# A mixer and MLP block on one core: tile 1's first product in two column halves, and another order of the work

## The chip, the cores and the metric

The kernel runs on one core of one Trainium2 chip. The metric is the device time of one execution in microseconds (us), the median over several runs; lower is better. A core has five engines that run side by side and meet at semaphores: TensorE (PE, matrix products and transposes into PSUM), VectorE (DVE), ScalarE (ACT, activations), GpSimd (POOL) and SyncE (SP, which issues most DMAs here). PEld in a profile is TensorE's loading of weights.

## The reference

With S = 2048 tokens, D = 512 and F = 1792, all in bf16:

```python
h = _gelu(_layernorm(x, axis=-1) @ w1)
c = D // 4
g0 = jnp.pad(h[:, :, 0*c:1*c], ((0, 0), (1, 0), (0, 0)))[:, :S, :]
g1 = jnp.pad(h[:, :, 1*c:2*c], ((0, 0), (0, 1), (0, 0)))[:, 1:, :]
g2 = jnp.pad(h[:, :, 2*c:3*c], ((0, 0), (2, 0), (0, 0)))[:, :S, :]
g3 = jnp.pad(h[:, :, 3*c:   ], ((0, 0), (0, 2), (0, 0)))[:, 2:, :]
hs = jnp.concatenate([g0, g1, g2, g3], axis=-1) @ w2
x1 = x + hs
h2 = _gelu(_layernorm(x1, axis=-1) @ w3) @ w4
return x1 + h2
```

Each quarter of h's columns is shifted by 1, -1, 2 or -2 tokens before the second product. A layer norm comes ahead of the first and of the third product. The tanh form of gelu is used.

## The kernel before

The tokens are cut into 16 tiles of 128. Everything stays in on-chip memory between loading and storing; x and the four weights are loaded once.

Per tile there are two layer norms, numbered q: q = 0 to 15 for the first (of x), q = 16 to 31 for the second (of x1, tile q-16). Statistics come from VectorE (L409, L411) or, for q in STAT_ACT, from ScalarE (L388, L393) with small VectorE steps (L398 to L405). GpSimd raises the variance to the power -0.5 (L416, rstd). The normalisation is done by VectorE (L437), by ScalarE (L446) or by GpSimd (L449), as the table NORM says; the last two need a factor nmr first (L442, placed by NMR). The normalised tile is then turned, to have its columns on the partitions: by TensorE with a copy out of PSUM (`pe_transpose`, L482 and L490, the copy placed by EVAC) or by a DMA transpose on SP's queue (L455).

The products, by the names that the order uses:

- up1: first product and gelu, for a group of tiles (GROUPS[1]). In general (L586, L601) the result has tokens along the free dimension, as the shifts need it. Tiles 0 and 1 (NAT) are done the other way round: the product is by rows (`mm_up_rows`, L520, x's tile as weights), a gelu with rstd as its scale (L539) writes hn, and TensorE turns hn (`h_transpose`, L557), from which it is copied to hT (L563, engine by HEV). So these tiles' products need not wait for rstd. Tile 0 (SPLIT) has its first half of the normalised columns turned and multiplied before the second: steps sa, sb and ra, rb, where the halves are of the contraction, not of the output.
- mix: the shifted second product (L626) and x1 = x + hs (L633 or L637). Mix t needs h of tiles t-1, t and t+1.
- up2: third product and gelu for a group of tiles (GROUPS[2], L586 and L601).
- down: fourth product (L655), addition of x1 (L663) and output DMA (L666). The last tile goes in three pieces (TAIL).

The third product of a tile needs the second layer norm of that tile, and that needs its mix. PSUM is used as three pairs of banks (y_ps: up1, up2, most transposes) and two single banks (o_ps: mix, down, h_transpose), each taken in turn.

The order of TensorE's work is written out in SCRIPT ("ty" is a TensorE transpose by number q, "th" the transpose of hn, "up2:0" a group's number). The order of the loads is written out in LOADS: "x4-5" is a DMA of two tiles, "a" and "b" are halves of a weight's rows, "@act" is issued by ScalarE, "tp11" is a DMA transpose with a fixed place among the loads, which counts only if TensorE does not do that transpose. For the other engines a planner (`order`, `place`) gives each step a due time, counted back from TensorE's order (starting at DUE, with BIAS added), and places the steps by a model of durations, waits and landings. The outcome is a fixed list for each engine; at run time each instruction waits for semaphores only, and an engine takes its list in order.

Of the kernel before, what the change touches and what calls it, by code (L numbers as in the profile page):

```python
# [6 lines left out]
P = 128  # L7
ACT_F = mybir.ActivationFunctionType
# [17 lines left out]
class Program:  # L26
# [2 lines left out]

    HOP = {"pe": 200.0, "dve": 155.0, "act": 220.0, "pool": 120.0, "sp": 70.0}  # L30
    LOOK = {"dve": 300.0, "act": 300.0}
    DUE = 252723.0
    BEGIN = {"sp": 30.0, "act": 150.0, "pe": 400.0, "dve": 150.0, "pool": 450.0}
    ENTRY = 1900.0
    COLD, RESTART = 4300.0, 800.0
# [219 lines left out]
        self.seq = out  # L255
        return out

GROUPS = {1: (1, 1, 1, 1, 1, 1, 2, 2, 2, 2, 2), 2: (2, 2, 4, 4, 4)}
NORM = {4: "act", 5: "act", 6: "act", 10: "act", 11: "pool", 12: "pool", 13: "act", 15: "act", 18: "pool", 20: "pool", 21: "pool", 22: "pool", 24: "act", 28: "act", 30: "pool"}
EVAC = {1: "both", 2: "dve", 3: "dve", 7: "both", 9: "dve", 10: "both", 11: "both", 13: "both", 16: "dve", 17: "both", 19: "both", 20: "dve", 22: "both", 23: "dve", 24: "dve", 25: "dve", 28: "dve", 31: "dve"}  # L260
STAT_ACT = (1, 6, 8, 9, 12, 21, 22, 23, 27, 28, 29)
TAIL = (256, 128, 128)
NMR = {0: "pool", 1: "pool", 3: "pool", 5: "pool", 7: "pool", 9: "pool", 10: "pool", 12: "pool", 13: "pool", 14: "pool", 17: "pool", 18: "pool", 19: "pool", 21: "pool", 22: "pool", 23: "pool", 27: "pool", 30: "pool"}
NAT = (0, 1)
SPLIT = (0,)
HEV = {2: "dve", 5: "dve", 6: "dve"}
BIAS = {}
LOADS = """
x0 w1a w1b x4-5 w2b tp2 x3 w2a x6-7 w3b x8 w3a x1@act x9 x2@act x11 tp16 w4a x10 tp11 w4b tp9 x12-14 x15
"""  # L270
SCRIPT = """
warm:8 sa:0 sb:0 ty:1 ra:0 rb:0 up1:1 ty:2 th:0-1 up1:2 mix:0 ty:4 ty:3 mix:1 up1:3 ty:5 up1:4 mix:2 up1:5
mix:3 ty:17 mix:4 up2:0 up1:6 up2:1 mix:6 down:1 mix:5 up1:7-8 mix:8 mix:7 up1:9 mix:10 down:0 down:2 mix:9
up1:10 mix:12 mix:11 up2:2 mix:13 down:3 down:6 mix:14 up2:3 mix:15 down:4-5 down:7 down:11 down:9-10 up2:4
down:8 down:12 down:14 down:13 down:15
"""

def bass_standalone__mixer_s_mlp__prompt_kernel(nc, x, w1, w2, w3, w4, out):
    B, S, D = x.shape
    F = w3.shape[1]  # L280
    assert B == 1 and D == 4 * P and S % 512 == 0 and F % (2 * P) == 0 and S >= 1024
    NT, DC, FC = S // P, D // P, F // P
# [10 lines left out]
    with ExitStack() as es:  # L293
        sb = lambda name, shape, dt: es.enter_context(nc.sbuf_tensor(name, shape, dt))
        x_sb = sb("x_sb", [P, NT, D], BF16)
        x1_sb = sb("x1_sb", [P, NT, D], BF16)
        xnT = sb("xnT", [P, DC, S], BF16)
        hT = sb("hT", [P, DC, HTW], BF16)
        h2T = sb("h2T", [P, FC, S], BF16)
        w1_sb = sb("w1_sb", [P, DC, D], BF16)  # L300
# [3 lines left out]
        ident = sb("ident", [P, P], BF16)  # L304
# [26 lines left out]
        def pair_rv(p, v):  # L331
            return [(("y", p, 0), v), (("y", p, 1), v)]
# [180 lines left out]
        def mm_up_rows(t):  # L513
            p, v = next_pair()
            k = NAT.index(t)

            def part(c0, c1):
                def f(e):
                    for dc in range(c0, c1):
                        ins = e.matmul(y_ps[:, p, 0:D], xnT[:, dc, P * t : P * (t + 1)], w1_sb[:, dc, :],  # L520
                                       start=(dc == 0), stop=(dc == DC - 1))
                    return ins

                return f

            if t in SPLIT:
                for hh in (0, 1):
                    cs = range(2 * hh, 2 * hh + 2)
                    pg.add("pe", f"rows{t}_{hh}", part(2 * hh, 2 * hh + 2),
                           reads=[(("w1", c), 0) for c in cs] + [(("xT", t, c), 1) for c in cs],  # L530
                           writes=[pair_rv(p, v)[hh]], dur=2 * 215.8)
                    if hh == 0:
                        yield
            else:
                pg.add("pe", f"rows{t}", part(0, DC),
                       reads=[(("w1", c), 0) for c in range(DC)] + [(("xT", t, c), 1) for c in range(DC)],
                       writes=pair_rv(p, v), dur=DC * 215.8)
            pg.add("act", f"gelur{t}",
                   lambda e: e.activation(hn[:, k, :], y_ps[:, p, 0:D], ACT_F.Gelu_apprx_tanh,  # L539
                                          scale=rstd[:, t : t + 1]),  # L540
                   reads=pair_rv(p, v) + [(("rstd", t), 0), (("warm",), 1)], writes=[(("hn", t), 0)], dur=50 + D * 0.833)
            yield

        def h_transpose(t, pair):
            g = group_of[1, t]
            how = HEV.get(t, "act")
            k = NAT.index(t)
            if pair:
                b, v = next_pair()
                res, dst = pair_rv(b, v), y_bf[:, b, 0:D]  # L550
            else:
                b, v = next_bank()
                res, dst = [(("o", b), v)], o_bf[:, b, 0:D]

            def f(e):
                for c in range(DC):
                    ins = e.transpose(dst[:, P * c : P * (c + 1)], hn[:, k, P * c : P * (c + 1)], ident[:])  # L557
                return ins

            pg.add("pe", f"th{t}", f, reads=[(("hn", t), 0), (("ident",), 1)], writes=res, dur=225)  # L560
            to, frm = hT[:, :, 2 + P * t : 2 + P * (t + 1)], dst.rearrange("p (c s) -> p c s", s=P)
            pg.add(how, f"evh{t}",
                   (lambda e: e.activation(to, frm, ACT_F.Copy)) if how == "act" else  # L563
                   (lambda e: e.tensor_copy(to, frm)),
                   reads=res, writes=[(("h", j, g), 0) for j in range(DC)],
                   dur=(60 + 0.82 * D) if how == "act" else (75 + 0.51 * D))


        def mm_up(layer, g):
            t0, n = groups[layer][g]  # L570
# [34 lines left out]
        def run(gen):  # L605
            for _ in gen:
                pass
# [82 lines left out]
        for step in SCRIPT.split():  # L690
            kind, n = step.split(":")
            a, _, b = n.partition("-")
            steps += [(kind, n) for n in (range(int(a), int(b or a) + 1) if kind != "warm" else [int(n)])]
        steps = [s for s in steps if s[0] not in ("th", "tz") or s[1] in NAT]
        pe_tp = {n for kind, n in steps if kind in ("tp", "ty", "sa")}
        queues = {"sp": [], "act": []}
        for i, item in enumerate(LOADS.split()):
# [10 lines left out]
        for kind, n in steps:  # L708
            if kind == "warm":
                warm_pe(n)  # L710
            elif kind in ("sa", "ra"):
                halves[kind[0], n] = pe_transpose(n, n, True) if kind == "sa" else mm_up_rows(n)
                next(halves[kind[0], n])
            elif kind in ("sb", "rb"):
                next(halves[kind[0], n])
            elif kind in ("tp", "ty"):
                run(pe_transpose(n % NT, n, kind == "ty"))
            elif kind in ("th", "tz"):
                h_transpose(n, kind == "tz")
            elif kind == "mix":  # L720
                mm_mix(n)
            elif kind == "down":
                mm_down(n)
            else:
                for _ in mm_up(int(kind[2]), n):
                    pass
# [103 lines left out]
```

## Time and profile before

| | us |
|---|---|
| median of 4 runs | 135.76 |
| the 4 runs | 135.68, 135.37, 135.84, 135.90 |
| the profiled execution | 135.68 |
| its span in the trace | 134.3 |

Busy times by stretch of the span, in us:

| stretch | PE | PEld | DVE | ACT | POOL | GB/s moved |
|---|---|---|---|---|---|---|
| 0 to 5 | 4.36 | 1.95 | 2.55 | 3.33 | 1.66 | 234 |
| 5 to 10 | 4.61 | 2.70 | 3.84 | 3.82 | 2.16 | 378 |
| 10 to 15 | 5.00 | 3.87 | 4.84 | 4.55 | 1.91 | 256 |
| 15 to 20 | 5.00 | 3.78 | 4.73 | 4.70 | 3.06 | 226 |
| 20 to 25 | 5.00 | 4.47 | 4.33 | 2.77 | 3.40 | 143 |

How to read it: the profile shows one execution. An engine's busy time is that of its instructions; the ends of matmuls are modelled, and a matmul overlaps the next, so a matmul's own length in the timeline is longer than the time by which it moves the next one. In the timeline a line gives the start, the length, engine, line of the code, operation, output and inputs with their shapes, how many instructions are merged in the line, and in square brackets the idle time before it and what ended it. The chain of waits goes back from the last instruction to what released each step. TensorE's clock was granted in full throughout (1.0).

Landings of the loads, each as issue plus time to landing in the trace, in us: x0 2.5, x1 2.8, x2 4.3, w1b 5.8, x4-5 6.5, w2b 7.2, x3 7.5, w2a 8.2, x6-7 9.0, w3b 11.2, w3a 13.9.

### The profile page before, as it was taken

How to read it: one execution, taken by the hardware profiler on the slowest of the kernel's cores; microseconds unless marked ns; L12 is line 12 of the kernel's file. 1: busy time of each engine (PE TensorE's matmuls, PEld its weight loads, DVE VectorE, ACT ScalarE, POOL GpSimd, SP SyncE). 2: the span in 40 equal slices, each digit the busy share in tenths (PEclk: the TensorE clock that was granted, in tenths of full speed). 3: DMA queues.
4: the chain of work that ended last, by engine and by line, in shares of the span. 5: the costliest groups of instructions: out<-in, count | busy, mean ns of one | idle time of the engine just before them, and what ended most of it. 6: DMA issues, size and time to landing. Idle time of an engine off the chain costs nothing.

```text
span 134.3 us, 2025 instructions
## 1 busy us (share of the span) xinstructions
PE 131.4 (98%) x792; PEld 72.8 (54%) x792; DVE 52.0 (39%) x140; ACT 58.4 (43%) x90; POOL 25.8 (19%) x59
## 2 busy tenths in 40 slices
PE   8989999999999999999999999999999999999994
PEld 3468688885576446444444444444444444444463
DVE  3889999404947737700053500062222200012222
ACT  5698995669394303775520366600000155520000
POOL 2534467600865301300010310010000000000000
PEclk9999999999999999999999999999999999999999
DMA  6999399599057532111003110004112100001112
GB/s 187 347 388 362 60 299 160 105 289 239 6 111 82 118 79 77 39 39 39 5 0 78 39 39 0 0 0 85 39 39 72 45 0 0 0 5 39 39 39 78
DMA packets 21897, 12.32 MB, mean 92 GB/s; under 512 B 14464, under 2 KB 21376, under 8 KB 21888
## 3 DMA queue, kind: packets, MB, share of 16 engines
q1 hardware_dynamic: 21168, 11.80, 33.6%
q10 hardware_dynamic: 720, 0.39, 1.0%
q8 instruction: 6, 0.10, 0.3%
q14 instruction: 3, 0.02, 0.0%
HBM read 6.82 MB, written 2.10 MB: 66 GB/s over the span
## 4 chain that ended last, share of the span: by engine, by line
PE 98%; ACT 1%; DVE 0%; issue 0%; POOLq 0%; ACTq 0%
PE y_ps L586 45%; PE o_ps L655 36%; PE o_ps L626 10%; PE o_ps L679 3%; PE y_ps L520 2%; PE y_ps L482 1%; ACT hn L539 1%; PE o_ps L557 0%; DVE o_sb L663 0%; POOLq L815 0%; ACTq L779 0%
## 5 line engine op out<-in xcount | busy, mean ns | idle before, releaser
L586 PE MATMUL y_ps<-xnT,w_sb 128*128 128x256 bf16 (+2 forms) x424 | 62.6, 307 | 0.0
L586 PEld LDWEIGHTS y_ps<-xnT,w_sb 128*128 128x128 bf16 x424 | 39.0, 98 | 23.4 <-DVE xnT L490 0.3
L655 PE MATMUL o_ps<-w_sb,h2T 128*128 128x512 bf16 (+2 forms) x252 | 49.2, 355 | 0.0
L601 ACT ACTIVATE h2T<-y_ps 128x1024 bf16<-128x1024 f32 (+1 forms) x29 | 28.6, 993 | 42.6 <-PE y_ps L586 42.6
L655 PEld LDWEIGHTS o_ps<-w_sb,h2T 128*128 128x128 bf16 x252 | 23.6, 98 | 25.2
L663 DVE TENSOR_TENSOR o_sb<-o_ps,x_sb 128x512 bf16<-128x512 f32 (+2 forms) x18 | 11.4, 632 | 40.0 <-PE o_ps L655 39.8
L416 POOL TENSOR_TENSOR rstd<-mv,neghalf 128x1 f32<-128x1 f32 x21 | 11.6, 554 | 42.6 <-DVE mv L411 38.6
L626 PE MATMUL o_ps<-w_sb,hT 128*128 128x512 bf16 x64 | 16.1, 379 | 0.0
L409 DVE BATCH_NORM_STATS2 st<-x_sb 128x6 f32<-128x512 bf16 x21 | 14.2, 675 | 2.2 <-DMA x_sb<-in_x_dram 2.0
L637 DVE TENSOR_TENSOR x_sb<-o_ps,x_sb 128x512 bf16<-128x512 f32 x10 | 6.9, 686 | 12.7 <-PE o_ps L626 12.7
L633 DVE SCALAR_TENSOR_TENSOR x_sb<-o_ps,x_sb 128x512 bf16<-128x512 f32 x6 | 4.1, 690 | 16.8 <-PE o_ps L626 16.8
L601 ACT ACTIVATE hT<-y_ps 128x1024 bf16<-128x1024 f32 (+1 forms) x9 | 7.4, 826 | 6.3 <-PE y_ps L586 6.2
L416 POOL TENSOR_TENSOR rstd<-vpe,neghalf 128x1 f32<-128x1 f32 x11 | 6.0, 549 | 18.8 <-DVE vpe L405 18.7
L626 PEld LDWEIGHTS o_ps<-w_sb,hT 128*128 128x128 bf16 x64 | 6.0, 98 | 5.5
L437 DVE TENSOR_SCALAR xn_buf<-x_sb,mv,rstd 128x512 bf16<-128x512 bf16 x15 | 7.0, 468 | 4.8 <-POOL rstd L416 4.6
L446 ACT ACTIVATE xn_buf<-x_sb,nmr,rstd 128x512 bf16<-128x512 bf16 x8 | 6.5, 811 | 5.2 <-DVE nmr L442 3.2
L393 ACT ACTIVATE junk<-x_sb 128x512 bf16<-128x512 bf16 x11 | 6.8, 622 | 2.7 <-DVE x_sb L633 2.7
L449 POOL TENSOR_SCALAR xn_buf<-x_sb,rstd,nmr 128x512 bf16<-128x512 bf16 x7 | 5.3, 763 | 0.8 <-DVE nmr L442 0.4
L679 PE MATMUL o_ps<-zeros 128*128 128x512 bf16 x8 | 3.6, 630 | 0.6 <-POOLq L815 0.6
L411 DVE BATCH_NORM_AGGREGATE mv<-st 128x2 f32<-128x9 f32 x21 | 4.0, 191 | 0.2
L388 ACT ACTIVATE junk<-x_sb 128x512 bf16<-128x512 bf16 x5 | 3.1, 622 | 0.3 <-DMA x_sb<-in_x_dram 0.3
L482 PEld LDWEIGHTS y_ps<-ident,xn_buf 128*128 128x128 bf16 x28 | 2.3, 111 | 1.3 <-issue 0.6
(35 smaller groups left out, 30.7 us busy)
## 6 DMA issues: line engine op xcount, KB each, us to landing
w_sb<-in_w_dram SPq DMA_DIRECT2D x4, 896.0 KB, 6.6
out_dram<-o_sb SPq DMA_DIRECT2D x15, 128.0 KB, 1.7
w_sb<-in_w_dram SPq DMA_DIRECT2D x4, 256.0 KB, 4.9
x_sb<-in_x_dram SPq DMA_DIRECT2D x7, 128.0 KB, 5.3
x_sb<-in_x_dram SPq DMA_DIRECT2D x2, 256.0 KB, 5.2
xnT<-xn_buf SPq DMA_TRANSPOSE x25, 2.5
x_sb<-in_x_dram SPq DMA_DIRECT2D x1, 384.0 KB, 4.9
x_sb<-in_x_dram ACTq DMA_DIRECT2D x2, 128.0 KB, 3.2
```

Source lines behind the costliest of these rows:

```text
L393: (lambda d: (lambda e: e.activation(d, src, ACT_F.Square, accum_out=sums[:, q, 1:2])))(junk[:, b, :]),
L409: pg.add("dve", f"bnst{q}", lambda e: e.bn_stats(st9[:, q, 0:6], src), reads=rs, writes=[(("st", q), 0)], dur=605)
L416: lambda e: e.tensor_tensor(col(rstd), var, neghalf[:], ALU.pow),
L437: lambda e: e.tensor_scalar(dst, src, mv[:, q, 0:1], rstd[:, q : q + 1], ALU.subtract, ALU.mult),
L446: f = lambda e: e.activation(dst, src, ACT_F.Identity, bias=nmr[:, q : q + 1], scale=rstd[:, q : q + 1])
L586: ins = e.matmul(y_ps[:, p, W * i : W * (i + 1)], wsb[:, dc, P * fc : P * (fc + 1)], src[:, dc, P * t0 : P * t0 + W], start=(dc == 0), sto ...
L601: (lambda d, s: (lambda e: e.activation(d, s, ACT_F.Gelu_apprx_tanh)))(dst, ysrc),
L626: ins = e.matmul(dst, hT[:, j, c0 : c0 + P], w2_sb[:, j, :], start=(j == 0), stop=(j == DC - 1))
L637: f = lambda e: e.tensor_tensor(x1_sb[:, t, :], dst, x_sb[:, t, :], ALU.add)
L655: ins = e.matmul(dst, h2T[:, fc, P * t : P * (t + 1)], w4_sb[:, fc, cs], start=(fc == 0), stop=(fc == FC - 1))
L663: (lambda d, c: (lambda e: e.tensor_tensor(o_sb[:, oi, c], d, x1_sb[:, t, c], ALU.add)))(dst, cs),
L679: ins = e.matmul(o_ps[:, b, :], zeros[:, 0:P], zeros[:], start=True, stop=True)
```

## The change

Two things are changed. The first is in the code: the new table CSPLIT holds tile 1. For it, the row product is done in two halves of its output columns, 256 each, over the whole contraction; each half lies in its own PSUM bank, has its own gelu, its own two transposes of hn (now in a pair of banks, half a pair each) and its own copy to hT. The steps "ra", "rb" do the halves of the product and gelu, the new steps "ta", "tb" those of the transpose and copy. Tile 0 keeps its form.

The second is the data of the plan: all tables, the order of the loads, TensorE's order and the starting time DUE are others. Some of what differs:

- TensorE transposes tiles 0 to 4 of layer norm 1 and tile 1 of layer norm 2 (q = 17); before also tile 5.
- Groups of the first product: 0, 1, 2, 3, 4, 5-6, 7-8, 9-10, 11-12, 13, 14-15 (before 0, 1, 2, 3, 4, 5, 6-7, ..., 14-15). Groups of the third product: 0, 1, 2-5, 6-7, 8-11, 12-15 (before 0-1, 2-3, 4-7, 8-11, 12-15).
- The third product of tile 1, then of tile 0, comes after mix 3; all of the first products and most mixes stand between them and the third product of tiles 2 to 5. The first down step comes after that. Before, the third product began after mix 4 with tiles 0-1, and a down step followed mix 6.
- All of x is loaded ahead of w4, and w4 stands behind the DMA transpose of q = 24. w2 and w3 are one DMA each. w3 stands behind x6.
- The copy of tile 0's h is done by VectorE, before by ScalarE; the copy of tile 1's transposed x by ScalarE alone, before by both.

```diff
-    DUE = 252723.0
+    DUE = 359495.0
...
-GROUPS = {1: (1, 1, 1, 1, 1, 1, 2, 2, 2, 2, 2), 2: (2, 2, 4, 4, 4)}
+GROUPS = {1: (1, 1, 1, 1, 1, 2, 2, 2, 2, 1, 2), 2: (1, 1, 4, 2, 4, 4)}
...
+NORM = {3: "pool", 5: "pool", 7: "pool", 10: "pool", 13: "act", 15: "pool", 18: "act", 20: "act", 21: "pool", 23: "pool", 24: "act", 25: "act", 27: "act", 29: "pool", 31: "act"}
+EVAC = {2: "dve", 5: "both", 9: "both", 11: "both", 12: "dve", 14: "dve", 16: "dve", 17: "both", 20: "dve", 23: "both", 24: "dve", 25: "both", 26: "dve", 29: "dve", 30: "dve", 31: "both"}
+STAT_ACT = (1, 6, 10, 12, 19, 21, 22, 25, 30)
...
+CSPLIT = (1,)
+HEV = {0: "dve", 3: "dve", 4: "dve", 5: "dve", 6: "dve"}
+BIAS = {"bnst2": 1142}
 LOADS = """
-x0 w1a w1b x4-5 w2b tp2 x3 w2a x6-7 w3b x8 w3a x1@act x9 x2@act x11 tp16 w4a x10 tp11 w4b tp9 x12-14 x15
+x0 w1a w1b x3 x1@act w2 x2@act x4 tp4 x7 tp4 tp3 x5 x6 w3 x15 x8-11 x12-14 tp24 w4a w4b
 """
 SCRIPT = """
-warm:8 sa:0 sb:0 ty:1 ra:0 rb:0 up1:1 ty:2 th:0-1 up1:2 mix:0 ty:4 ty:3 mix:1 up1:3 ty:5 up1:4 mix:2 up1:5
-mix:3 ty:17 mix:4 up2:0 up1:6 up2:1 mix:6 down:1 mix:5 up1:7-8 mix:8 mix:7 up1:9 mix:10 down:0 down:2 mix:9
-up1:10 mix:12 mix:11 up2:2 mix:13 down:3 down:6 mix:14 up2:3 mix:15 down:4-5 down:7 down:11 down:9-10 up2:4
-down:8 down:12 down:14 down:13 down:15
+warm:8 sa:0 sb:0 ty:1 ra:0 rb:0 ra:1 rb:1 ty:2 th:0 ta:1 tb:1 up1:2 mix:0 ty:3 mix:1 ty:4 up1:3-4 mix:2
+ty:17 mix:3 up2:1 up1:5 up2:0 mix:5 mix:4 up1:6-7 mix:7 up1:8 mix:9 mix:8 up1:10 mix:6 mix:10 up1:9 mix:11
+mix:15 up2:2 mix:12 down:0 down:3 down:2 mix:14 up2:3 down:1 up2:4 mix:13 down:6-7 down:10 up2:5 down:4
+down:8 down:5 down:11 down:9 down:13-14 down:12 down:15
 """
...
+            if t in CSPLIT:
+                H = D // 2
+                for hh in (0, 1):
+                    cs = slice(H * hh, H * (hh + 1))
+
+                    def f(e, hh=hh, cs=cs):
+                        for dc in range(DC):
+                            ins = e.matmul(y_ps[:, p, 512 * hh : 512 * hh + H], xnT[:, dc, P * t : P * (t + 1)],
+                                           w1_sb[:, dc, cs], start=(dc == 0), stop=(dc == DC - 1))
+                        return ins
+
+                    pg.add("pe", f"rows{t}_{hh}", f,
+                           reads=[(("w1", c), 0) for c in range(DC)] + [(("xT", t, c), 1) for c in range(DC)],
+                           writes=[pair_rv(p, v)[hh]], dur=DC * 109.2)
+                    pg.add("act", f"gelur{t}_{hh}",
+                           (lambda a, b: (lambda e: e.activation(a, b, ACT_F.Gelu_apprx_tanh,
+                                                                 scale=rstd[:, t : t + 1])))(
+                               hn[:, k, cs], y_ps[:, p, 512 * hh : 512 * hh + H]),
+                           reads=[pair_rv(p, v)[hh], (("rstd", t), 0), (("warm",), 1)], writes=[(("hn", t, hh), 0)],
+                           dur=50 + H * 0.833)
+                    yield
+                return
...
+            if t in CSPLIT:
                 b, v = next_pair()
+                steps = [(2 * hh, 2 * hh + 2, [pair_rv(b, v)[hh]], f"_{hh}") for hh in (0, 1)]
+                dst = y_bf[:, b, :].rearrange("p (k x) -> p k x", k=2)[:, :, 0 : D // 2]
+                chunk = lambda c: dst[:, c // 2, P * (c % 2) : P * (c % 2 + 1)]
+                part = lambda c0, c1: dst[:, c0 // 2, :].rearrange("p (c s) -> p c s", s=P)
             else:
                 b, v = next_bank()
+                steps = [(0, DC, [(("o", b), v)], "")]
+                dst = o_bf[:, b, 0:D]
+                chunk = lambda c: dst[:, P * c : P * (c + 1)]
+                part = lambda c0, c1: dst.rearrange("p (c s) -> p c s", s=P)
+            for c0, c1, res, tag in steps:
+                def f(e, c0=c0, c1=c1):
+                    for c in range(c0, c1):
+                        ins = e.transpose(chunk(c), hn[:, k, P * c : P * (c + 1)], ident[:])
+                    return ins
...
+                yield
```

## The prediction, made before the changed kernel had run

> **What bounds the kernel now.** I read the busy shares first, then the chain of waits in order of time, then the timeline of the first 20 us on all engines, then the DMA issues in narrow windows, for single landings.
>
> ```profile
> PE 131.4 (98%) x792; PEld 72.8 (54%) x792; DVE 52.0 (39%) x140; ACT 58.4 (43%) x90; POOL 25.8 (19%) x59
> ```
>
> The chain of waits shows where the missing 2% are (start, length, what):
>
> ```profile
> 0.65 3.59 PE o_ps L679 x8
> 4.24 0.85 PE y_ps L482 x8
> 5.09 2.20 PE y_ps L520 x8
> ...
> 7.37 0.69 ACT hn L539
> 8.07 0.05 issue
> 8.11 0.40 PE o_ps L557 x4
> 8.51 0.89 PE y_ps L586 x16
> 9.40 0.91 PE o_ps L626 x4
> ...
> 17.34 13.97 PE y_ps L586 x128
> ...
> 117.29 15.19 PE o_ps L655 x98
> ```
>
> From 8.51 to the end of TensorE at 132.49 no other engine is on the chain. Is that stretch dense, or are small stalls hidden in it? I add up its work by rates that the chain gives: 55.8 ns for a 128-column matmul (0.89/16), 109.1 for 256 columns (13.97/128), 215.9 for 512 (12.09/56). First products of tiles 2 to 5 4x0.893, five doubles 5x1.746, four transposed tiles 4x0.223, mixes 16x0.863, third product 2x6.11+3x12.09, down 15x3.02+3.09: 123.9 us, against 123.98 there. So nothing can be gained after 8.5 us except by less TensorE work, and everything that comes late is a loss. What is left is the start; its timeline:
>
> ```profile
> 5.77 1.01 PEld L520 LDWEIGHTS y_ps<-w_sb,xnT 128*128 128x128 bf16 x6 [0.64 <-DMA w_sb<-in_w_dram]
> 6.51 0.69 ACT L539 ACTIVATE hn<-y_ps,rstd 128x512 bf16<-128x512 f32 x1 [1.00 <-PE y_ps L520]
> 7.37 0.69 ACT L539 ACTIVATE hn<-y_ps,rstd 128x512 bf16<-128x512 f32 x1 [0.17 <-PE y_ps L520]
> 8.11 0.40 PE L557 MATMUL o_ps<-ident,hn 128*128 128x128 bf16 x4 [0.39 <-ACT hn L539]
> 8.35 1.06 PE L586 MATMUL y_ps<-xnT,w_sb 128*128 128x128 bf16 x16
> ```
>
> TensorE waits twice: until 5.77 for the second half of w1, and until 8.11 for tile 1's gelu, a single ACTIVATE which itself waited for the whole of tile 1's product.
>
> **What the Trainium skill says.** "ScalarE: Activation LUTs", section "What ACT_TABLE_LOAD costs": 0.833 ns per element on a fixed part, more for a pointer operand, and back-to-back ACTIVATEs overlap by about 93 ns. The trace agrees: 687 ns for 512 columns with the scale pointer, 585 without; the copy at 7.96 starts 0.10 before the gelu ends. "TensorE: Matmul & The Clock Gate", "Back-to-back issue gap": about 81 ns per 128-column matmul in a sustained stream with weight loads. The trace disagrees for 16 in a row (55.8); 56 in a row it does not show. "DMA: Bandwidth & Descriptors", "Queues, rings and completion order": each DMA engine consumes descriptors in ring order. This trace has a case: the transpose at 24.73, issued right behind w4b, landed 6.0 us later, against 2.5 for the median.
>
> **The change part by part.** *Tile 1's halves.* w1b's landing does not move: only x0, x1, x2, w1a stand ahead of it in both. So tile 0's product still ends at 6.3 and its gelu runs 6.51 to 7.20. Before, tile 1's product was done for ScalarE at 7.37. Now half 0 ends at 6.3+0.44 plus 0.2 of latency (the gap before 6.51), about 6.95, before ScalarE is free; half 1 at 7.4. A half gelu is 687-256x0.833 = 474 ns, and the next can start 0.10 before it ends. So the gelus run 6.51, 7.10, 7.48 and end at 7.95, against 8.06. One instruction more, but its fixed part fits into the 0.17 that ScalarE waited. The last two transposes start at 8.00 and take 0.11 instead of 0.22, so up1:2 starts at 8.13 instead of 8.35: **-0.22**. Bounds: 0 if VectorE's copy of tile 0's h (now there, 0.42) goes ahead of tile 2's copy, which up1:2 needs; -0.49 if TensorE never waits after 5.87: product 1.30, tile 2 0.22, h 0.45, together until 7.84. Mix 0 at 9.02 needs the h copies: tile 1's are done by 8.7, w2 (now one load, earlier in the queue) by 7.6. Both hidden.
>
> *TensorE work.* One tile fewer (5) is transposed by TensorE: -0.22. Third product of tiles 0 and 1 singly: 112x55.8 ns = 6.25 for 6.11, +0.14. Tile 1's product in halves: 8x109.1 for 4x215.8, +0.01. Sum **-0.07**; with 81 ns, the skill's figure, the 112 matmuls would give +2.8 more.
>
> *The order.* The third product comes earlier: up2:1 after 6.83 us of listed work, at 14.95 (before: up2:0 at 17.34). I go through what it needs.
> (a) w3, now in one piece. Data to its end 3.93 MB; the DMA rates by the microsecond add up to that at 12.1, and before's loads landed 1.4 after their bytes: 13.5. Hidden with 1.4 to spare.
> (b) ty:17, reached at 13.83, needs layer norm 2 of tile 1, mix 1 ending at 10.96. The shortest such chain in the trace, mix end to normalised tile (VectorE, start and length):
>
> ```profile
> 50.84 0.69 DVE L637 TENSOR_TENSOR x_sb<-o_ps,x_sb 128x512 bf16<-128x512 f32 x1 [0.17 <-PE o_ps L626]
> 51.56 0.69 DVE L409 BATCH_NORM_STATS2 st<-x_sb 128x6 f32<-128x512 bf16 x1
> 52.29 0.20 DVE L411 BATCH_NORM_AGGREGATE mv<-st 128x2 f32<-128x9 f32 x1
> 53.22 0.41 DVE L437 TENSOR_SCALAR xn_buf<-x_sb,mv,rstd 128x512 bf16<-128x512 bf16 x1 [0.73 <-POOL rstd L416]
> ```
>
> 50.80 to 53.63 plus a hop: 2.88, so 13.84: no slack at all. In the crowded early stretch, VectorE 4.84 of 5 us busy, the same chain took 3.44 (11.62 to 15.06), unharmed since ty:17 came at 16.09. Behind ty:17 TensorE's queue holds mix 3, up2:1 and all else. So the stall is 0 to 0.56; I take **+0.15**, as this chain is now the urgent one on VectorE while a normalisation on GpSimd (0.76) can still block its rstd.
> (c) ty:3, ty:4 and their copies: x3 lands at 6.1 instead of 7.5, x4 at 7.9 instead of 6.5; by the durations above ty:4's tile is ready at 10.2 for 10.96, its copy at 11.8 for 12.07. Hidden; x4 late by 0.7 would show.
> (d) up1:5, at 18.07, needs the DMA transposes of tiles 5 and 6. All x is now queued on SP ahead of them: 4.98 MB before the first transpose, against 4.33. The bytes are through at 14.8; the transposes follow 0.6 apart and land at about 16.8 and 17.4. Hidden, with 0.7 to spare; tile 16's, due at 19.8, likewise.
> From 20 us on there is more slack: first products until 38.8, with VectorE's work for them (about 19 us by my count of rows) in 24 us; w4, behind the transpose of tile 24 on SP, is issued at about 35 and needed at 51.8. The tail is the same order of kinds, with the same last pieces.
>
> **Sum.** The profiled execution took 135.68, its span 134.3 and 1.38 around it: 135.68-0.22-0.07+0.15 = 135.54. It lies 0.08 under the median of 135.76, so 135.6 for the median.
>
> **Rivals.** A measurement tells 0.3% (0.41 us) from no change: below 135.35, above 136.17.
> 1. *TensorE free from 5.87 on and no stall after*: 135.76-0.49-0.07 = 135.2. For it: GpSimd and ScalarE are idle around 7. Against: the gelu of tile 0 alone holds ScalarE till 7.1, and two halves end no earlier than 7.95; it needs w1b earlier too.
> 2. *A transfer takes the place of the wait* (the slower side): the transposes of tiles 5 and 6 sit in SP's ring behind 1 MB of x that up1:5 doesn't need. Were tile 6's, issued at about 13.5, to take 6.0 as the one behind w4b did, it would land at 19.5 and stall TensorE 1.4: 137.0. It decides from a landing at 18.65, 0.55 beyond the predicted sum. Against: that one landed 0.6 after its load, which is what I used.
> 3. *ty:17 late by both a VectorE and a GpSimd collision*: 0.56 to 1.1 instead of 0.15: 136.0 to 136.6.
> 4. *56 small matmuls in a row at 81 ns*: 138.4. Against: the 16s show no such growth.
>
> **How the numbers follow.** Forecast, 135.6 with its own range 135.2 to 136.0: 0.47, of which 0.05 below 135.35 and 0.01 above 136.17. Rival 1: 0.21. Rival 2: 0.18. Rival 3: 0.11, of which 0.02 within. Rival 4: 0.03. Faster 0.26, within 0.43, slower 0.31. The range reaches from 135.1 (rival 1) to 136.9, most of rival 2; what lies outside is rival 4 and the ends of 1 and 2.
>
> **What would show it.** Right: up1:2's first matmul near 8.13 and two gelus of about 0.47 each for tile 1; the third product at 55.8 ns in its first 112 matmuls; the chain of waits on TensorE alone from there on, but for a piece of VectorE or GpSimd near 13.8. Wrong: a DMA transpose on the chain near 18, w3 on it near 15, or a start that does not move, because VectorE's new copy holds up tile 2.

## The result

| | before | after |
|---|---|---|
| median, us | 135.51 (64 runs, 135.00 to 137.97) | 135.98 (43 runs, 135.37 to 137.72) |
| ratio after / before, 95% | | 1.0032 (1.0020 to 1.0045) |
| median span, us | 134.2 | 134.5 |
| median time around the span, us | 1.33 | 1.39 |
| the profiled execution, its span | 135.68, 134.3 | 135.41, 134.1 |

The changed kernel is slower by 0.3% (0.47 us in the median). The forecast was a slight gain: 0.14 on the profiled execution. Spans of before are those of 152 runs that were measured beside the experiments below; the 64 come without spans. Ratios are of mean times, without the executions that lie more than 1.5% above the fastest of their kernel (one of each here). Two things about the numbers. The four runs shown of before had a median of 135.76; 64 runs put it at 135.51, so the starting point was 0.25 too high. And the one execution of after that was profiled is a lucky one: at 135.41 it lies near the lowest of 43, while before's, at 135.68, lies above the median of its 64. Compared by themselves, these two profiles would say "0.27 faster", the wrong sign. What follows therefore rests on further executions of both kernels.

First the profile of after. The busy shares, as in the prediction:

```profile
PE 131.5 (98%) x848; PEld 73.7 (55%) x848; DVE 52.1 (39%) x139; ACT 55.7 (42%) x84; POOL 26.2 (20%) x58
```

TensorE is as full as before. The timeline of ScalarE, then of TensorE, around tile 1's halves and after:

```profile
6.32 0.69 ACT L562 ACTIVATE hn<-y_ps,rstd 128x512 bf16<-128x512 f32 x1 [0.61 <-PE y_ps L521]
6.90 0.83 ACT L542 ACTIVATE hn<-y_ps,rstd 128x256 bf16<-128x256 f32 x2
...
7.43 0.65 PE L587 MATMUL y_ps<-ident,hn 128*128 128x128 bf16 x4
7.91 1.06 PE L619 MATMUL y_ps<-xnT,w_sb 128*128 128x128 bf16 x16
...
12.81 1.02 PE L659 MATMUL o_ps<-w_sb,hT 128*128 128x512 bf16 x4
13.82 0.40 PE L483 MATMUL y_ps<-ident,xn_buf 128*128 128x128 bf16 x4
14.05 1.03 PE L659 MATMUL o_ps<-w_sb,hT 128*128 128x512 bf16 x4
14.91 8.29 PE L619 MATMUL y_ps<-xnT,w_sb 128*128 128x128 bf16 x128
```

The wait of 0.39 for tile 1's single gelu is gone; two half gelus take 0.83 together and up1:2 starts at 7.91, against 8.35. Between mix 2 (12.81) and ty:17 (13.82) lie 1.01 us. The same pair in the timeline of before lies 0.87 apart:

```profile
15.22 1.03 PE L626 MATMUL o_ps<-w_sb,hT 128*128 128x512 bf16 x4
16.09 0.39 PE L482 MATMUL y_ps<-ident,xn_buf 128*128 128x128 bf16 x4
```

So there is a gap of 0.14 in after, and no bracket names it, being so short. The chain of waits then shows the third product's start and up1:5:

```profile
13.84 0.38 PE y_ps L483 x4
14.21 0.86 PE o_ps L659 x4
15.08 8.12 PE y_ps L619 x128
...
104.97 27.28 PE o_ps L688 x154
```

The 128 matmuls are up2:1 and up2:0 (together 112 of 128 columns, 55.8 ns each) with up1:5 between them (16 of 256 columns, 109.1 ns): 6.25+1.75 = 8.00. They took 8.12, so a second small gap is hidden in one merged row.

### The profile page after: what moved, and what is told of

Its sections match the earlier page's. It is cut to its first block, busy times and chain, and to the rows that moved or that the text cites. A ratio compares the mean times of both kernels' runs of the same rounds, so it can differ in the third digit from the quotient of the medians.

```text
span 134.1 us, 2122 instructions
## 1 busy us (share of the span) xinstructions
PE 131.5 (98%) x848; PEld 73.7 (55%) x848; DVE 52.1 (39%) x139; ACT 55.7 (42%) x84; POOL 26.2 (20%) x58
## 4 chain that ended last, share of the span: by engine, by line
PE 93%; DMA 3%; DVE 1%; SPq 1%; ACT 1%; POOL 0%; issue 0%
PE y_ps L619 46%; PE o_ps L688 36%; PE o_ps L659 10%; DMA x_sb<-in_x_dram 3%; SPq L373 1%; ACT hn L542 1%; PE y_ps L483 1%; DVE st L410 1%; POOL rstd L417 0%; SPq L366 0%; DVE xn_buf L438 0%; DVE o_sb L696 0%; PE y_ps L587 0%; DVE mv L412 0%; SPq L849 0%
## 5 line engine op out<-in xcount | busy, mean ns | idle before, releaser
L619 PE MATMUL y_ps<-xnT,w_sb 128*128 128x128 bf16 (+2 forms) x480 | 62.9, 290 | 0.0
L619 PEld LDWEIGHTS y_ps<-xnT,w_sb 128*128 128x128 bf16 x480 | 39.9, 98 | 22.8
L634 ACT ACTIVATE h2T<-y_ps 128x1024 bf16<-128x1024 f32 (+2 forms) x29 | 28.7, 993 | 30.8 <-PE y_ps L619 30.8
L417 POOL TENSOR_TENSOR rstd<-mv,neghalf 128x1 f32<-128x1 f32 x23 | 12.7, 554 | 45.6 <-DVE mv L412 41.2
L410 DVE BATCH_NORM_STATS2 st<-x_sb 128x6 f32<-128x512 bf16 x23 | 15.6, 678 | 2.0 <-DMA x_sb<-in_x_dram 1.9
L394 ACT ACTIVATE junk<-x_sb 128x512 bf16<-128x512 bf16 x9 | 5.6, 624 | 11.7 <-DVE x_sb L666 11.7
L417 POOL TENSOR_TENSOR rstd<-vpe,neghalf 128x1 f32<-128x1 f32 x9 | 5.1, 566 | 13.3 <-DVE vpe L406 13.3
L450 POOL TENSOR_SCALAR xn_buf<-x_sb,rstd,nmr 128x512 bf16<-128x512 bf16 x8 | 6.2, 778 | 1.1 <-DVE nmr L443 0.8
L447 ACT ACTIVATE xn_buf<-x_sb,nmr,rstd 128x512 bf16<-128x512 bf16 x7 | 5.6, 805 | 0.0
L491 ACT ACTIVATE xnT<-y_ps 128x256 bf16<-128x256 bf16 (+1 forms) x6 | 2.8, 487 | 1.2 <-PE y_ps L483 1.2
```

The source lines that it names most:

```text
L394: (lambda d: (lambda e: e.activation(d, src, ACT_F.Square, accum_out=sums[:, q, 1:2])))(junk[:, b, :]),
L410: pg.add("dve", f"bnst{q}", lambda e: e.bn_stats(st9[:, q, 0:6], src), reads=rs, writes=[(("st", q), 0)], dur=605)
L417: lambda e: e.tensor_tensor(col(rstd), var, neghalf[:], ALU.pow),
L447: f = lambda e: e.activation(dst, src, ACT_F.Identity, bias=nmr[:, q : q + 1], scale=rstd[:, q : q + 1])
L450: f = lambda e: e.tensor_scalar(dst, src, rstd[:, q : q + 1], nmr[:, q : q + 1], ALU.mult, ALU.add)
L619: ins = e.matmul(y_ps[:, p, W * i : W * (i + 1)], wsb[:, dc, P * fc : P * (fc + 1)], src[:, dc, P * t0 : P * t0 + W], start=(dc == 0), sto ...
```

## The experiments

Each run below has a median of its own and a ratio to before from runs on the same chip; a run of a single execution has one time. To see where time goes I use one measure for all profiles: from up1:2's first matmul to the start of the last addition (VectorE, the last line of the kernel's work). It leaves out the start, and while TensorE has no gap it is a constant: 124.16 in the profile of before, where the chain has none, and 124.16-0.07 = 124.09 for after, by the predicted change of work. What is above that is gaps.

**Both kernels again, unaltered.** No edit. Labels again (timed), again_2, again_3, again_4 and before_2, before_3 (one profiled execution each).

> The changed kernel unaltered, for a second profile and its spread. All theories: 0.3% slower than before (ratio 1.002 to 1.0045). The profile so far is of an execution of 135.41, at the fast end of the runs (median 135.98), so about 0.5 us of a usual execution is not in it. A second profile of a usual run should show that 0.5 us as idle TensorE. Theory A (start): between 6 and 8 us, ahead of ty:2, since VectorE's list has tile 3's statistics ahead of tile 2's normalisation, so that x3's landing (5.14 in the first profile) holds tile 2 up. Theory B (ty:17): a gap at 13.8 of more than the 0.16 of the first profile. Theory C (transposes): a gap ahead of up1:5 near 18.2, where tile 6's transpose landed 0.1 to 0.2 ahead of need.

> The changed kernel unaltered, one more profile. Theory C: if the execution is a slow one (above 135.9), the gap is ahead of up1:5 near 18.3, from tile 6's transpose; if it is fast (below 135.6), that transpose lands before 18.3. Theory D: ty:17 starts 5.8 us after tile 4's statistics begin, in both.

> The kernel before, unaltered, one look. Theory (the new order hangs on landings that the old one doesn't): whatever the start gives, TensorE shows no gap over 0.1 us between 8.5 us and its end; the time from up1:2's first matmul to the last VectorE addition stays at 124.1 to 124.4 us (124.16 in the profile shown). Rival (the old order is exposed alike, and its one profile was a lucky one): a gap of 0.2 us or more at ty:17 or at up1:5, and 124.5 or more.

> The kernel after, unaltered, one look. Theory: ty:17 starts 5.7 to 5.9 us after tile 4's statistics begin and up1:5 waits for tile 6's transpose wherever that lands later than about 18.2; the time from up1:2's first matmul to the last addition is 124.4 to 125.5 us, and grows with the landing of tile 4 and of tiles 8 to 14. Rival (start gain carried, loss elsewhere): 124.1 to 124.3 as the sum of the work gives.

> As before_2: 124.1 to 124.4 us from up1:2's first matmul to the last addition, whatever the start; under the rival 124.5 or more with a gap at ty:17 or up1:5.

> As again_3: 124.4 to 125.5 us from up1:2's first matmul to the last addition, with the difference to 124.1 found in gaps at ty:17 and at up1:5; under the rival 124.1 to 124.3.

Measured: again 136.3 (135.51 to 137.0, 11 runs), ratio 1.0053 (1.0029 to 1.0077). The profiles, in us:

| profile | its time | tile 0's gelu starts | up1:2 starts | last addition starts | up1:2 to last addition | gap at ty:17 | gaps elsewhere |
|---|---|---|---|---|---|---|---|
| before | 135.68 | 6.51 | 8.35 | 132.51 | 124.16 | 0 | 0 |
| before_2 | 135.92 | 6.78 | 8.62 | 132.78 | 124.16 | 0 | 0 |
| before_3 | 135.42 | 6.28 | 8.11 | 132.28 | 124.17 | 0 | 0 |
| after | 135.41 | 6.32 | 7.91 | 132.27 | 124.36 | 0.14 | 0.13 |
| again | 135.74 | 6.02 | 7.61 | 132.59 | 124.98 | 0.55 | 0.34 |
| again_2 | 137.11 | 6.59 | 8.18 | 133.68 | 125.50 | 0.20 | 1.21 |
| again_3 | 135.66 | 5.97 | 7.57 | 132.50 | 124.93 | 0.13 | 0.71 |
| again_4 | 135.34 | 6.08 | 7.68 | 132.17 | 124.49 | 0.13 | 0.27 |

(Gap at ty:17: distance from mix 2's row less 0.87. The last column is the time from up1:2 to the last addition less 124.09 and less that gap.)

Before is rigid: three executions with starts 0.5 us apart, one time from up1:2 to the last addition to 0.01 us. Its start passes through to the end whole, and nothing after it comes late. After starts earlier by 0.57 in the mean (8.36 against 7.79). Of this, 0.24 is the halves: from tile 0's gelu to up1:2 it is 1.83 to 1.84 us in all three profiles of before and 1.59 to 1.60 in all five of after. The rest, 0.33, is that tile 0's gelu itself starts earlier (6.52 against 6.20 in the mean). But after's gaps are 0.27 to 1.41, 0.76 in the mean. The expectation for again_3 and again_4 (124.4 to 125.5) held, and its rival, a carried start with a loss elsewhere (124.1 to 124.3), fell; so did the rival that before's profile was a lucky one. One thing expected of again_3 and again_4 did not hold as put: up1:5 waited there for tile 6's transpose although that landed at 18.03 and 17.94, not later than 18.2, because TensorE came to it sooner (17.69 and 17.81, and 0.14 pass between the landing and the first matmul).

The timeline of TensorE in again_2 has the largest gap:

```profile
15.25 3.29 PE L619 MATMUL y_ps<-xnT,w_sb 128*128 128x128 bf16 x56
19.57 4.64 PE L619 MATMUL y_ps<-xnT,w_sb 128*128 128x256 bf16 x65 [1.04 <-DMA xnT<-xn_buf]
```

and the chain of waits in again_2 leads to it:

```profile
12.29 0.77 POOL xn_buf L450
13.06 1.08 POOL rstd L417 x2
...
14.16 0.41 DVE xn_buf L438
...
14.61 4.83 DMA xnT<-xn_buf
19.44 0.14 issue
19.57 5.03 PE y_ps L619 x72
```

GpSimd normalises tile 5 (0.77), then raises the variances of q = 17 and of tile 6 to their power (two in 1.08), VectorE normalises tile 6, and its DMA transpose, issued at 14.61, lands after 4.83. What did it cost? The bracket says 1.04, but it counts from the modelled end of the last matmul before the gap. By the rates the 56 matmuls move the next one by 56x55.8 ns = 3.13, so up1:5 could have started at 15.25+3.13 = 18.38; it started at 19.57. That is 1.20 of the 1.21. The 72 matmuls behind the gap lose nothing more: in again_3 they start at 18.17 and the next product at 23.04, 4.87 later, which is what the rates give (16x109.1+56x55.8). The 5.03 in the chain includes the tail of the last matmul.

How the landing depends on the loads ahead of it, from the DMA issues (issue plus time to landing):

| profile | x12-14 lands | tile 6's transpose issued | lands | up1:5 could start | lost at up1:5 |
|---|---|---|---|---|---|
| again_4 | 16.8 | 14.04 | 17.94 | 17.81 | 0.27 |
| after | 16.9 | 14.27 | 18.03 | 18.04 | 0.13 |
| again_3 | 16.9 | 13.92 | 18.03 | 17.69 | 0.48 |
| again | 17.2 | 14.53 | 18.36 | 18.30 | 0.19 |
| again_2 | 18.3 | 14.61 | 19.44 | 18.38 | 1.20 |

"Could start" is the start of up2:1 plus 3.13. The landing plus 0.14, less that, gives the loss in all five to 0.01. Over these five, tile 6's transpose lands 1.1 after the load x12-14, whatever its issue. again_3 issued it 0.35 sooner than after, and it landed at the same time: TensorE's lead of 0.35 was lost there. again and again_2 issued it within 0.1 of each other, and it landed 1.1 apart, as x12-14 did. So the x load in front decides, not the issue. (no_halves, below, is an exception.)

Most of again's own loss was elsewhere. TensorE there, by its timeline:

```profile
12.65 1.03 PE L659 MATMUL o_ps<-w_sb,hT 128*128 128x512 bf16 x4
14.07 0.40 PE L483 MATMUL y_ps<-ident,xn_buf 128*128 128x128 bf16 x4 [0.40 <-DVE xn_buf L438]
```

The start was at 7.61, ty:17 at 14.07. VectorE began tile 4's statistics at 8.34 there, after standing 0.53 us for x4's landing, and in after at 8.02, without a wait, with ty:17 at 13.82. In nine of the other eleven profiles on the new plan, too, ty:17 comes 5.7 to 5.9 after that instruction (6.0 and 6.1 in the rest), so VectorE's list from there on paces this step. x4's landing adds to it only where VectorE has to wait for it. Where it did not (after, again_3, again_4), ty:17 came 5.90 to 5.91 after up1:2's start, and only the 0.13 to 0.14 was lost.

**The halves alone, on before's plan** (halves_only; the other engines' lists held as before):

```diff
 (before's tables, loads and DUE, with the new code)
+CSPLIT = (1,)
-... ra:0 rb:0 up1:1 ty:2 th:0-1 up1:2 ...
+... ra:0 rb:0 ra:1 rb:1 ty:2 th:0 ta:1 tb:1 up1:2 ...
```

> The kernel before with only the halves of tile 1 added, every other engine's list as it was. If the halves are worth what the prediction said: 0.2 us faster than before, ratio 0.9985. Theory A, B and C all put the loss in the plan and not in the halves, so all say at most 1.000.

Measured: 135.57 (135.03 to 136.27, 22 runs), ratio 1.0005 (0.9990 to 1.0021); span 134.2 in the median, as before. Timelines of ScalarE and TensorE in halves_only:

```profile
6.43 0.69 ACT L605 ACTIVATE hn<-y_ps,rstd 128x512 bf16<-128x512 f32 x1 [0.92 <-PE y_ps L564]
...
8.03 1.06 PE L662 MATMUL y_ps<-xnT,w_sb 128*128 128x128 bf16 x16
9.03 1.02 PE L702 MATMUL o_ps<-w_sb,hT 128*128 128x512 bf16 x4
9.89 0.75 PE L526 MATMUL y_ps<-ident,xn_buf 128*128 128x128 bf16 x8
```

up1:2 starts 1.60 after tile 0's gelu, as in after, and 0.32 sooner than in the profile of before (0.08 of it because that gelu is earlier). But from there mix 0 starts 1.00 later (0.94 before), and ty:4 with ty:3 takes 0.75 (0.61): the steps behind are late now. From up1:2 to the last addition it is 124.36 there, 0.20 above before. So the halves do bring TensorE forward, and within two or three steps the next inputs (mix 0's copies, the tiles for ty:3 and ty:4) hand most of it back. The -0.22 of the halves was measured as +0.07 (-0.14 to +0.28).

**The new plan without the halves** (no_halves; other lists held):

```diff
-CSPLIT = (1,)
+CSPLIT = ()
-... ra:1 rb:1 ty:2 th:0 ta:1 tb:1 up1:2 ...
+... up1:1 ty:2 th:0-1 up1:2 ...
```

> The changed kernel with tile 1's halves undone (one product of 512 columns, one gelu, four transposes into a single bank, one copy); every other engine's list as in the changed kernel. If the halves are worth what the prediction said: 0.22 us slower than the changed kernel, ratio to before 1.005. If a usual execution hides them behind tile 2 being late (theory A): less than 0.1 us slower. If the halves are what costs: faster.

Measured: 136.71 (135.96 to 136.98, 6 runs), ratio 1.0088 (1.0063 to 1.0113). Its profile (136.66) has the wait for tile 1's gelu again (0.39 at 7.81), and the same stall as again_2, in its timelines of ScalarE and TensorE:

```profile
6.21 0.69 ACT L604 ACTIVATE hn<-y_ps,rstd 128x512 bf16<-128x512 f32 x1 [0.50 <-PE y_ps L563]
...
7.81 0.40 PE L629 MATMUL o_ps<-ident,hn 128*128 128x128 bf16 x4 [0.39 <-ACT hn L604]
8.05 1.06 PE L661 MATMUL y_ps<-xnT,w_sb 128*128 128x128 bf16 x16
...
19.41 0.81 PE L661 MATMUL y_ps<-xnT,w_sb 128*128 128x256 bf16 x6 [1.03 <-DMA xnT<-xn_buf]
```

Without the halves up1:2 starts 1.84 after tile 0's gelu, as in before, so their 0.24 at the start is shown on both plans. What they are worth at the end on the new plan is not settled. Against after's 1.0032 the difference is 0.0056, 0.76 us; against again, measured in the same series as no_halves, it is 0.0035, 0.47 us, and by the two intervals anything up to twice that or nearly nothing. So that the halves save more than their 0.24 is not shown. The one profile of no_halves has a bracket of 1.03 at the transpose; whether the halves change that landing or it fell out so, the runs don't tell. Why tile 6's transpose took 4.83 here, though x12-14 had landed at 16.6, the trace does not show.

**Tile 2's normalisation first** (norm2_first). VectorE's list has tile 3's statistics ahead of tile 2's normalisation; that is turned round:

```diff
+MOVE = [('bnst3', 'norm2')]   # put behind it in its engine's list
```

> The changed kernel with one step moved: tile 3's statistics (bnst3) after tile 2's normalisation on VectorE, as the kernel before has its next statistics. All other lists as they are. Theory A: 0.2 to 0.4 us faster than the changed kernel, ratio to before about 1.000, since x3's landing no longer stands ahead of tile 2. Theories B and C: no change beyond 0.1 us, ratio 1.003; it could lose 0.1 by later statistics of tile 3, which have 0.9 us to spare.

Measured: 135.76 (135.19 to 137.25, 14 runs), ratio 1.0023 (0.9995 to 1.0052), span 134.2 in the median. It is the best of the new plan's variants, but its interval also holds after's 1.0032 and meets that of again (1.0053), measured in the same series, so the gain isn't established. ty:17 still waited 0.24 in its profile.

**The x loads moved.** Three runs that take one exposure away each, or several:

```diff
 x12_late:     +MOVE = [('dma_x12', 'tp6')]      x12-14 behind the transposes of tiles 5 and 6
 x4_early:     +MOVE = [('dma_w2', 'dma_x4')]    x4 ahead of w2
 three_moves:  +MOVE = [('bnst3', 'norm2'), ('dma_x12', 'tp6'), ('dma_w2', 'dma_x4')]
```

> The changed kernel with one DMA moved: the load of x12-14 is issued after the DMA transposes of tiles 5 and 6 instead of ahead of them; all else as it is. Theory C (the transposes of tiles 5 and 6 land late behind 384 KB of x that is not needed yet; tile 6's landed at 19.3 in the profile without halves, and held up1:5 for 1.1 us): tile 6's transpose lands about 1 us earlier relative to its issue (2.5 to 3 us instead of 3.8 to 4.8), and the median falls by 0.3 to 0.5 us, ratio to before about 1.000, the spread too. Theory D (the vector chain from x4's landing to ty:17, 5.8 us in all four profiles, sets the pace): no change beyond 0.1 us.

> The changed kernel with one DMA moved: x4 ahead of w2 instead of behind it. Theory D (ty:17 comes 5.8 us after x4's landing, whatever the start does): x4 lands at about 6.9 instead of 8.2, ty:17 starts when TensorE reaches it, at 13.5 to 13.7, with no gap; 0.2 to 0.5 us faster than the changed kernel. It gives tile 6's transpose an earlier issue too. w2 comes 0.35 later, at 7.9 for a need at 8.6. Theory C alone: less than 0.2 us.

> The changed kernel with three moves: tile 3's statistics after tile 2's normalisation, x4 ahead of w2, x12-14 behind the transposes of tiles 5 and 6. If C and D each hold their part: TensorE dense from 8 us on in a usual execution, 0.5 to 0.7 us faster than the changed kernel, ratio to before 0.998 to 0.9995. If neither: 1.003.

Measured, 22 runs each: x12_late 136.18, ratio 1.0044 (1.0027 to 1.0062); x4_early 136.03, 1.0033 (1.0015 to 1.0051); three_moves 136.02, 1.0042 (1.0021 to 1.0062). None is better than after, so the gains that were expected (0.2 to 0.7 us) did not come. The TensorE timeline says why. x12_late:

```profile
14.27 0.40 PE L496 MATMUL y_ps<-ident,xn_buf 128*128 128x128 bf16 x4 [0.36 <-DVE xn_buf L451]
...
20.97 3.29 PE L632 MATMUL y_ps<-xnT,w_sb 128*128 128x128 bf16 x56 [0.56 <-ACT junk L402]
```

Tile 6's transpose now landed 2.5 after its issue, as expected, at 17.95, and up1:5 did not wait. But x12-14 landed at 20.2, and up2:0 waited. The bracket names ScalarE's sum of tile 12 (L402), which ended at 20.96. It was hardly that: in three_moves up2:0 starts at 20.30, before that sum ends (20.34). Tile 16's transpose, behind x12-14 in the queue, landed at 20.84, 0.13 ahead of the first matmul, and that fits. ty:17 lost time too, as VectorE stood 0.88 for x4. three_moves names the transpose of tile 16 itself:

```profile
20.30 3.29 PE L632 MATMUL y_ps<-xnT,w_sb 128*128 128x128 bf16 x56 [0.42 <-DMA xnT<-xn_buf]
```

In x4_early x4 landed at 6.0, but VectorE came to its statistics at 7.89 and then stood 0.51 for x5, which landed later than in after (9.3 against 8.6). ty:17 started at 13.98, no sooner than in after, so an early x4 alone does not free this step. The timelines of VectorE and TensorE:

```profile
9.31 0.69 DVE L423 BATCH_NORM_STATS2 st<-x_sb 128x6 f32<-128x512 bf16 x1 [0.51 <-DMA x_sb<-in_x_dram]
...
13.98 0.40 PE L496 MATMUL y_ps<-ident,xn_buf 128*128 128x128 bf16 x4
...
18.65 5.03 PE L632 MATMUL y_ps<-xnT,w_sb 128*128 128x256 bf16 x72 [0.28 <-DMA xnT<-xn_buf]
```

The last line is the transpose of tile 6 again. One wait is taken away, and the next in line shows.

**The whole of tile 12 moved back**, so that neither transpose nor gelu stands behind x12-14; alone (x12_behind_tp16), and with tile 2 first and x4 early (x12_behind_tp16_start):

```diff
+MOVE = [('dma_x12', 'tp16'), ('sum12', 'gelu2_0_0'), ('ssq12', 'sum12'), ('msq12', 'x1_5'), ('vpe12', 'msq12'),
+        ('norm12', 'x1_4'), ('rstd12', 'norm15'), ('tp12', 'tp14')]
 (x12_behind_tp16_start adds ('bnst3', 'norm2') and ('dma_w2', 'dma_x4'))
```

> The changed kernel with the load of x12-14 moved behind the DMA transposes of tiles 5, 6 and 16, and the steps on tile 12 moved to where that load can serve them (ScalarE's two statistics after the gelu of up2:0's first piece, the VectorE and GpSimd steps behind). In x12_late the transposes landed at 16.5 and 17.6, early enough, but ScalarE waited at its list for x12 (landed 20.3), and behind that stood a gelu, 0.56 us of TensorE. Theory C (the tail of the x loads, landing between 16.9 and 18.3 over five profiles, is what holds the transposes of tiles 5 and 6, and so up1:5): no gap ahead of up1:5 over 0.1 us, none ahead of up2:0; median 0.3 to 0.5 us below the changed kernel, ratio to before 0.999 to 1.001, and fewer executions above 136.3 (before them: a quarter). If it stays at 1.003, the loss is elsewhere.

> The same with two moves more: tile 3's statistics after tile 2's normalisation on VectorE, and x4 loaded ahead of w2. If ty:17 (0.16 to 0.55 us of gap in the profiles) costs on top of the transposes: another 0.2 us, ratio to before 0.997 to 0.999, and faster than both kernels. If GpSimd's normalisation of tile 5, which stands ahead of tile 17's rstd (as in x4_early's profile), takes over: no gain over the run without the two moves.

Measured: 136.06 (16 runs), ratio 1.0029 (1.0011 to 1.0046); and 136.02 (22 runs), 1.0033 (1.0015 to 1.0051). The expectations (0.999 to 1.001 and 0.997 to 0.999) were missed. In both profiles the row of 128 matmuls runs without a gap from up2:1 through up1:5 to up2:0; the losses are before and behind it. The timeline of x12_behind_tp16 shows TensorE, then VectorE:

```profile
5.96 0.60 PE L534 MATMUL y_ps<-w_sb,xnT 128*128 128x512 bf16 x2 [0.47 <-DMA w_sb<-in_w_dram]
...
8.07 0.40 PE L496 MATMUL y_ps<-ident,xn_buf 128*128 128x128 bf16 x4 [0.64 <-DVE xn_buf L451]
...
16.01 8.16 PE L632 MATMUL y_ps<-xnT,w_sb 128*128 128x128 bf16 x128
...
29.23 1.03 PE L672 MATMUL o_ps<-w_sb,hT 128*128 128x512 bf16 x4
30.37 1.91 PE L632 MATMUL y_ps<-xnT,w_sb 128*128 128x256 bf16 x16
...
7.01 0.69 DVE L423 BATCH_NORM_STATS2 st<-x_sb 128x6 f32<-128x512 bf16 x1 [1.65 <-DMA x_sb<-in_x_dram]
7.62 0.40 DVE L451 TENSOR_SCALAR xn_buf<-x_sb,mv,rstd 128x512 bf16<-128x512 bf16 x1
```

Here x3 landed at 7.0 (5.1 in after). VectorE stood 1.65 us for tile 3's statistics with tile 2's normalisation next in its list, and TensorE waited 0.64 for tile 2. That exposure is a third one, in the list itself; norm2_first and the variant with it do not have it. That variant's profile waited 0.25 at ty:17 instead. And both have a new gap where tile 12 is needed: its transpose, moved back too, landed at 30.23 and 29.09, and up1:8 (tiles 11 and 12) lost 0.28 and 0.24; behind a mix of four matmuls a product otherwise starts after 0.86, here after 1.14. The execution profiled for x12_behind_tp16 took 136.68, against a median of 136.06; w1b and x3 landed late in it.

**Tiles 5 and 6 turned by TensorE** (tiles_5_6_on_pe), which takes the DMA transposes out of the question at a known price of two times 0.22:

```diff
-ty:17 mix:3 up2:1 up1:5 ...
+ty:17 mix:3 ty:5-6 up2:1 up1:5 ...
 (and copies ev5dve, ev5act, ev6 in the lists; other lists held)
```

> The changed kernel with tiles 5 and 6 transposed by TensorE after mix 3 instead of by DMA, so that up1:5 waits for no DMA transpose; other lists as they are. TensorE's work rises by 0.45 us. Theory C: the stall that goes is 0.1 us in the best executions and over 1.0 in the worst, so the fastest run is 0.3 to 0.4 slower than the changed kernel's fastest, the median the same within 0.2, and the upper tenth (136.6 there) falls. If C is wrong: everything 0.45 slower, ratio 1.0065.

Measured: 136.25 (135.37 to 137.43, 22 runs), ratio 1.0055 (1.0033 to 1.0076). Its profile has no gap at up1:5 (124.68 from up1:2 to the last addition, against 124.09+0.45+0.13 = 124.67 with the gap at ty:17 alone). It adds 0.45 of TensorE work and loses 0.0023 (about 0.3) against after, each measured beside its own runs of before. The difference of the two, roughly 0.15, is an estimate of what the transposes cost after, with an uncertainty of about 0.35. The expectation did not hold: the fastest run was not slower (135.37, as in after), the median rose by 0.27, not by less than 0.2, and the slowest tenth did not get faster (137.2 and more, against 136.8 and more). So the transposes are not the only source of after's longer times.

## Why the prediction was wrong

It foresaw nearly all the pieces. One was mis-sized, the landing ahead of up1:5, and one was taken for granted, that an earlier start is kept to the end. By its own steps:

- *Tile 1's halves, -0.22*: held, in mechanism and in size. They give 0.24 in all five profiles of after and in halves_only. Tile 0's gelu came 0.33 earlier besides, so up1:2's start moved by 0.57 in the mean. That goes against "w1b's landing does not move": w1b landed at 4.8 to 5.0 in the five profiles of after, and at 5.1 to 5.8 in the three of before. What moves it I did not try. So the larger gain at the start was luck, not foresight.
- *That this start is carried to the end.* The sum adds -0.22 to the end, as if the following steps had slack. On before's plan it is not carried: halves_only is worth +0.07 (-0.14 to +0.28), not -0.22. I had read "no other engine on the chain after 8.51" as "nothing else matters"; it says that nothing was late at before's pace, not by how little.
- *TensorE work, -0.07*: held. The gap at up1:5 in after is 0.12 by its row (8.12 for 8.00), so up1:2 to the last addition less both gaps is 124.36-0.14-0.12 = 124.10, for the predicted 124.09. The 56 small matmuls in a row stay at 55.8 ns: 3.13 for 56 in again's and again_4's chains. Rival 4 fell, and with it, for this kernel, the figure of 81 ns of the Trainium skill's page "TensorE: Matmul & The Clock Gate" ("Back-to-back issue gap").
- *(a) w3*: held; it landed at 13.5, the predicted figure, and is on no chain.
- *(b) ty:17, +0.15*: held in size. 0.13 to 0.55 in five profiles, 0.23 in the mean, inside the bounds of 0 and 0.56. The largest, in again, came from x4's landing.
- *(c) ty:3, ty:4*: held in after; x3 and x4 are not late for them. But x4 landed at 8.3 and 8.4 in again and again_2, for the predicted 7.9, and held up VectorE's list to ty:17 in again; and x3's landing is an exposure through VectorE's order (0.64 in x12_behind_tp16).
- *(d) the transposes of tiles 5 and 6, "Hidden, with 0.7 to spare"*: **this is the step that failed**, by its landing. The need, put at 18.07, came at 17.7 to 18.4, 18.04 in the mean. Tile 6's transpose was to land at 17.4; it landed at 17.9 to 19.4. So the 0.7 of slack was 0 in the best execution, and up1:5 lost 0.13 to 1.20, 0.45 in the mean of five profiles. The working can be followed to the term that was too small. Bytes through at 14.8, landing of the last x load 1.4 later, at 16.2, and the two transposes 0.6 apart behind it. By the packets in the traces of after, 98% of the bytes of these loads were through at 14.8 to 15.4, and the transposes came 0.5 and 1.1 behind x12-14, both nearly as predicted. But x12-14 landed at 16.8 to 18.3: their last packets ended only at 16.1 to 17.8. Counted from those 98%, the landing came 2.0 to 3.0 later, where 1.4, read from before's loads, had been put.

Rival 2 described just this, with place (tile 6 behind 1 MB of x), landing (19.5) and effect (137.0): again_2 is that case, 19.44 and 137.11. The parts differ: the transpose was issued at 14.61 and took 4.83, for 13.5 and 6.0, so that the landing agrees so closely is chance. The rival had a chance of 0.18, as an alternative to the forecast. In fact it comes on top of the forecast, by 0.1 to 1.2 from one execution to the next. Summed over the profiles, -0.57 at the start, -0.07 of work and +0.76 of gaps give +0.12, against a predicted -0.22-0.07+0.15 = -0.14.

The profiles' +0.12 is not the whole 0.47. The span is 0.30 longer over all runs (134.54 in the mean of 44, against 134.25 of 152). The three profiles of before are of executions 0.09 above that mean, the five of after 0.08 below, and this explains why they show only 0.12. The rest lies around the span: 1.39 against 1.33 in the median, but 1.53 against 1.32 in the mean, as 15 of after's 44 executions have over 1.5 (up to 2.8), where none of before's 152 went over 1.39. halves_only (at most 1.40 in 22) does not have them, and no_halves (1.38) not either, though six runs are few; all other variants of the new plan do. What it is stays open: the traces' starts and ends show no difference. Open, too, is why the last packets of the same x load end up to 1.7 us apart from one execution to the next. And no variant beats before: the best are halves_only, equal to it, and norm2_first. So that the gaps cost after its gain is shown for the executions that were profiled; that closing the gap at up1:5 would make it faster is not, as each variant that closed it lost elsewhere.

## What to carry to other kernels

A chain without waits tells that nothing was late in one execution, not how near it was; before moving TensorE's start forward, write down for each next input the landing, the need and the difference, and give the difference the spread of several executions. The landing of a load is that of its last packet: here 98% of the bytes were through on time, and the rest took 1.3 to 2.5 us more. Tile 6's transpose, behind such loads in its queue, landed 1.1 after the last of them, for issues from 13.9 to 14.6 (no_halves alone differs). Where a wait is removed and the time stays, look for the next in line: four variants here each closed the gap at up1:5 and showed another. And where a bracket names an engine, see whether another profile has the same step before that engine is done.

## What the runs showed of the hardware

- Landings vary from run to run by more than this change is worth: x12-14 took 10.8 to 12.1 us in five executions of one kernel, x3 3.6 in after and 5.5 in x12_behind_tp16.
- In again_2 the DMA engines moved 22 GB/s from 17 to 18 us and 230 from 18 to 19 (shares 0.07 and 1.11), while TensorE waited from 18.4; in after it was 148 and 39. A share of 0.07 is about one engine of 16 (0.06). The trace's packets agree: from 16.5 to 17.8 packets of the x loads end one by one, about 0.045 us apart, as from one engine, and 0.5 after the last of them x12-14 lands. So the last part of these loads, and the transposes behind them, hung on about one engine (an estimate from the share and the packets); why it was behind the trace does not say.
- The bracket of a TensorE stall is shorter than the time lost: 1.04 for 1.20 in again_2, as it counts from the modelled end of the last matmul. In again_3 the 72 matmuls after a stall took 4.87 to the next product, no more than the rates give.
- TensorE's first matmul came 0.13 to 0.14 after the landing of the DMA transpose that it waited for (again_2, again_3, again_4, three_moves).
- Three executions of before had the same 124 us to within 0.01, with loads that landed up to 0.7 apart: there the order had slack at each input, and the spread of the landings did not show after the start.
